# The gate and up products of a gated layer with the 64-row remainder of both weights side by side, and x^T by transposing DMAs

## The chip, the core and the metric

The kernel runs on one core of a Trainium2 chip. A core has engines with instruction streams of their own: TensorE (PE in the profile; its weight loads are PEld), VectorE (DVE), ScalarE (ACT), GpSimd (POOL) and SyncE (SP, which here only issues DMAs). They share the on-chip memory SBUF, with 128 partitions; TensorE writes its results to PSUM, 128 partitions by eight banks, each of which holds 512 f32 per partition. The metric is the device time of one execution in microseconds.

## The reference

The kernel computes an attention block with a cached K and V, multiplied by a gated layer, and all gradients. Cut to what matters here:

```python
x = A_x                                  # 1 x 2048 x 576
xn = _layernorm(x, axis=-1)
s = _A_ref(xn, k_cache, v_cache, wq, wo) # attention, 32 heads
def _B_ref(x, w_gate, w_up, w_down):     # 576 x 4608, 576 x 4608, 4608 x 576
    g = einsum("bsd,df->bsf", x, w_gate)
    u = einsum("bsd,df->bsf", x, w_up)
    h = sigmoid(g) * u
    return einsum("bsf,fd->bsd", h, w_down)
out = x + s * silu(_B_ref(xn, w_gate, w_up, w_down))
# returned: out and the gradients of x, k_cache, v_cache, wq, wo, w_gate, w_up, w_down
```

The change is in the first stage: the layer norm, xn transposed, g and u, and three results for later stages: a = sigmoid(g), h = a u, and b = h (1 - a), which the gradient needs.

## The kernel before

x has S = 2048 rows, 16 row tiles of 128 (`NT`); its D = 576 columns are four blocks of 128 and a remainder of 64 (`DT` = 5, `DL` = 4, `KL` = 64); the F = 4608 columns of Wg and Wu are nine chunks of 512 (`FCH`, `NFC`).

The first stage (lines 177 to 263 below):

- SP loads the first two tiles of x into `x_all`, the first chunk of `wg_sb` and `wu_sb` block by block of 128 rows, the other 14 tiles of x in one DMA (L197), then the further columns of both weights. `wg_sb` and `wu_sb` have five blocks each; of the fifth only 64 rows are data, and POOL zeroes the other 64 (`zpad`, L160), there and in `xnT`, so that every matmul uses all 128 rows.
- `ln_tile` (L206) normalizes a tile: statistics on DVE (L211, L213), the root on ACT (L215), its reciprocal and the bias on DVE, the normalization on ACT (L220), and then `transpose_to` (L53): five transposes on PE (L59), copied from PSUM to `xnT` by DVE (L42) and ACT (L40).
- The chunks run in three groups of three (`GRP`), within a group over the 16 tiles. For a tile and chunk there are five matmuls of 512 columns for g (L249) and five for u (L252); then two sigmoids of g on ACT (L253, L255) and two products on DVE (L256, L257). Each (tile, group) has three rows `a_row`, `b_row`, `h_row` that POOL stores by DMA to `a_d`, `b_d` and `h_d` (L259 to L263). PSUM holds three pairs of `g_ps` and `u_ps` (`a1ps`) and two banks for the transposes.
- POOL issues the store of xn and the load of `wd_sb`, the down projection's weights (L235, L236). `hT` of the first two tiles is read back from `h_d` by transposing DMAs in the last group (L261).

The order of instructions on each engine is the scheduler's here, not the program's: it may move an instruction ahead of others that it doesn't depend on. The load of `wd_sb`, for one, stands in the program at the last tile of the first group, and is issued 11 us into the execution.

The next stage (from L265) multiplies h by `wd_sb` (L306), with `hT` from transposing DMAs (`load_hT`, L279) into memory that the first stage's weights leave; `transpose_ds` (L266) later fills rows 64 to 127 of the last block of `xnT`. Much later a stage reads a, b and h again in blocks of columns (`load_abh`, L750) and computes another product with a 64-row remainder: `dh_main` (L782) and `dh_fifth` (L789), the latter with operands that alternate between rows 0 to 63 and 64 to 127.

Of the kernel before, what the change touches and what calls it, by code (L numbers as in the profile page):

```python
# [9 lines left out]
bf = mybir.dt.bfloat16  # L10
f32 = mybir.dt.float32
# [84 lines left out]
def kernel(  # L96
# [42 lines left out]
    a_d = dram.tile([S, F], bf, name="a_d")  # L139
    b_d = dram.tile([S, F], bf, name="b_d")  # L140
    h_d = dram.tile([S, F], bf, name="h_d")
# [9 lines left out]
    eps_t = pers.tile([P, 1], f32, name="eps_t")  # L151
    nc.vector.memset(eps_t[:], EPS)

    alt = Alt(nc)
    KPAD = dts[-1][1] < P
    d_last, kd_last = dts[-1]

    def zpad(t):
        if KPAD:
            nc.gpsimd.memset(t[kd_last:, DT - 1, :], 0.0)  # L160

    def kfull(i, kd):
        return P if KPAD else kd

    FCH = min(512, F)
    NFC = F // FCH
    GRP = ldiv(NFC, 3)
# [6 lines left out]
    zpad(xnT)  # L174
    dsT = pk.tile([P, DL, S], bf, name="dsT")
    wo_h = pk.tile([P, D], bf, name="wo_h")
    with tc.tile_pool(name="pa", bufs=1) as pa:
        wd_sb = pa.tile([P, FT, D], bf, name="wd_sb")
        with tc.tile_pool(name="a1w", bufs=1) as wp:
            a0x = tc.alloc_tile_pool(name="a0x", bufs=1, side="right")  # L180
            x_all = a0x.tile([P, NT, D], bf, name="x_all")
            XF = min(2, NT)
            nc.sync.dma_start(x_all[:, 0:XF, :], x2[0:XF * P, :].rearrange("(t p) d -> p t d", p=P))
            xn_st = x_all
            wg_sb = wp.tile([P, DT, F], bf, name="wg_sb")
            wu_sb = wp.tile([P, DT, F], bf, name="wu_sb")
            zpad(wg_sb)
            zpad(wu_sb)
            WSPL = GRP * FCH
            bounds = [0, FCH] + list(range(WSPL, F + 1, WSPL)) if WSPL > FCH else list(range(0, F + 1, WSPL))  # L190
            for bi in range(len(bounds) - 1):
                c0, c1 = bounds[bi], bounds[bi + 1]
                for i, (d0, kd) in enumerate(dts):
                    nc.sync.dma_start(wg_sb[:kd, i, c0:c1], B_w_gate[d0:d0 + kd, c0:c1])
                    nc.sync.dma_start(wu_sb[:kd, i, c0:c1], B_w_up[d0:d0 + kd, c0:c1])
                if bi == 0 and NT > XF:
                    nc.sync.dma_start(x_all[:, XF:, :], x2[XF * P:, :].rearrange("(t p) d -> p t d", p=P))  # L197
            FMAX = nc.vector.BN_STATS_FMAX
            nchunk = 1
            while D % nchunk != 0 or D // nchunk > FMAX:  # L200
                nchunk += 1
            with tc.tile_pool(name="a0", bufs=3) as sb0, tc.tile_pool(name="a0ps", bufs=2, space=PSUM) as ps0, \
                    tc.tile_pool(name="a1r", bufs=2) as rows, tc.tile_pool(name="a1t", bufs=3) as tmpp, \
                    tc.tile_pool(name="a1ps", bufs=3, space=PSUM) as ps:

                def ln_tile(st):  # L206
                    xt = x_all[:, st, :]
                    stats = sb0.tile([P, nchunk, nc.vector.BN_STATS_DIM], f32, name="stats")
                    xr = xt.rearrange("p (c f) -> p c f", c=nchunk)
                    for c in range(nchunk):  # L210
                        nc.vector.bn_stats(stats[:, c, :], xr[:, c, :])  # L211
                    mv = sb0.tile([P, nc.vector.BN_AGGR_DIM], f32, name="mv")
                    nc.vector.bn_aggr(mv[:], stats[:])  # L213
                    std = sb0.tile([P, 1], f32, name="std")
                    nc.scalar.activation(std[:], mv[:, 1:2], AF.Sqrt, bias=eps_t[:], scale=1.0)  # L215
                    nc.vector.reciprocal(rstd_all[:, st:st + 1], std[:])
                    xn_t = xn_st[:, st, :]
                    nbias = sb0.tile([P, 1], f32, name="nbias")
                    nc.vector.scalar_tensor_tensor(nbias[:], mv[:, 0:1], -1.0, rstd_all[:, st:st + 1], op0=ALU.mult, op1=ALU.mult)
                    nc.scalar.activation(xn_t, xt, AF.Identity, bias=nbias[:], scale=rstd_all[:, st:st + 1])  # L220
                    transpose_to(nc, ps0, xn_t, D, xnT, st * P, ident, alt)

                LA = 2
                for st in range(min(LA, NT)):
                    ln_tile(st)
                for grp in range(NFC // GRP):
                    if grp == 1:
                        a0x.release()
                        hp0 = tc.alloc_tile_pool(name="a2h0", bufs=1, side="right", reuse_waits="tile")
                        hT = {k: hp0.tile([P, FT, P], bf, name=f"hT{k}") for k in range(2)}  # L230
                    for st in range(NT):
                        if grp == 0 and st + LA < NT:
                            ln_tile(st + LA)
                        if grp == 0 and st == NT - 1:
                            nc.gpsimd.dma_start(xn_d[:, :].rearrange("(t p) d -> p t d", p=P), xn_st[:])  # L235
                            nc.gpsimd.dma_start(wd_sb[:], B_w_down.rearrange("(t p) d -> p t d", p=P))  # L236
                        srows = slice(st * P, (st + 1) * P)
                        a_row = rows.tile([P, GRP * FCH], bf, name="a_row")
                        b_row = rows.tile([P, GRP * FCH], bf, name="b_row")
                        h_row = rows.tile([P, GRP * FCH], bf, name="h_row")  # L240
                        for c in range(GRP):
                            fc = grp * GRP + c
                            fs = slice(fc * FCH, (fc + 1) * FCH)
                            cs = slice(c * FCH, (c + 1) * FCH)
                            g_ps = ps.tile([P, FCH], f32, name="g_ps")
                            u_ps = ps.tile([P, FCH], f32, name="u_ps")
                            for i, (d0, kd) in enumerate(dts):
                                kk = kfull(i, kd)
                                nc.tensor.matmul(g_ps[:], lhsT=xnT[:kk, i, srows], rhs=wg_sb[:kk, i, fs], start=(i == 0), stop=(i == DT - 1))  # L249
                            for i, (d0, kd) in enumerate(dts):  # L250
                                kk = kfull(i, kd)
                                nc.tensor.matmul(u_ps[:], lhsT=xnT[:kk, i, srows], rhs=wu_sb[:kk, i, fs], start=(i == 0), stop=(i == DT - 1))  # L252
                            nc.scalar.activation(a_row[:, cs], g_ps[:], AF.Sigmoid)  # L253
                            oma = tmpp.tile([P, FCH], bf, name="oma")
                            nc.scalar.activation(oma[:], g_ps[:], AF.Sigmoid, scale=-1.0)  # L255
                            nc.vector.tensor_tensor(h_row[:, cs], u_ps[:], a_row[:, cs], op=ALU.mult)  # L256
                            nc.vector.tensor_tensor(b_row[:, cs], h_row[:, cs], oma[:], op=ALU.mult)  # L257
# [766 lines left out]
```

## Time and profile before

| | |
|---|---|
| median of 3 runs | 5152.12 us (5147.52 to 5171.49) |
| the profiled execution | 5157.5 us as a run, 5155.7 us span |
| first matmul of g | 8.25 us |
| first matmul of the next stage (L306) | 349.16 us |
| TensorE busy, whole span | 4983.8 us, 97% |
| matmuls of g and u recorded (L249, L252) | 693 and 717 of 720 each |
| transposes of x on TensorE (L59) | 80 |

The profile is one execution. A row of a group of instructions gives the line, engine and operation, output and inputs with their shapes, the count, busy time and the mean length of one in ns, and then the idle time of the engine just before them and what ended it. A row of the order by time gives the start and length in us, and a count if equal instructions are merged. Matmuls are pipelined and overlap, so the pace is read from the distance of starts, not from the mean length. A DMA row gives the size and the median time from issue to landing.

### The profile page before, as it was taken

What the parts mean: (1) busy time and instruction counts of PE and PEld (TensorE: products, weight loads), DVE (VectorE), ACT (ScalarE), POOL (GpSimd) and SP (SyncE); (2) the same over time, 40 slices, a digit from 0 to 9 for tenths busy, and PEclk for the clock granted to TensorE, in tenths of its full rate; (3) what the DMA queues carried; (4) which work ended last, traced back from release to release, by engine and by line L of the source; (5) the groups of instructions that cost most, each with busy time, mean ns of one, the idle gap of its engine ahead of it and who ended that gap; (6) DMA issues with size and microseconds to landing.
All of it is one profiled execution on the core that took longest, in us unless ns stands there. A gap on an engine that the chain in (4) does not pass through costs nothing.

```text
span 5155.7 us, 124622 instructions
## 1 busy us (share of the span) xinstructions
PE 4983.8 (97%) x53232; PEld 3490.9 (68%) x54160; DVE 3231.5 (63%) x5070; ACT 2285.3 (44%) x2878; POOL 1388.1 (27%) x1981
## 2 busy tenths in 40 slices
PE   8999999999999999999999999999899999999999
PEld 3444777777777777777777777777655555554554
DVE  5545888888888888888888888888733222210101
ACT  6531665566556556655655665566501222100000
POOL 2222333233223323332332333233222222111000
PEclk9999999999999999999999999999999999999999
DMA  7478999999999999999999999999999776697775
GB/s 281 184 210 166 189 191 196 195 199 195 196 196 196 197 201 199 196 202 196 199 196 198 199 197 195 199 199 195 205 200 246 209 209 196 199 246 166 158 153 118
DMA packets 2710509, 1013.89 MB, mean 197 GB/s; under 512 B 2523360, under 2 KB 2643936, under 8 KB 2709952
## 3 DMA queue, kind: packets, MB, share of 16 engines
q1 hardware_dynamic: 2628256, 726.57, 81.9%
q0 software_dynamic: 81696, 279.29, 18.5%
q8 instruction: 423, 6.93, 0.5%
q14 instruction: 134, 1.10, 0.1%
HBM read 172.54 MB, written 201.00 MB: 72 GB/s over the span
## 4 chain that ended last, share of the span: by engine, by line
PE 84%; DVE 6%; DMA 5%; issue 4%; SPq 1%; ACT 0%; DVEq 0%; ACTq 0%; another core or an unknown queue 0%
PE acckv L544 17%; PE acc L525 14%; PE acc L965 8%; PE dp L495 6%; PE sp L465 5%; DVE sneg L467 5%; PE accp L424 5%; PE accw L848 5%; DMA dST<-dSq 3%; PE g_ps L249 3%; PE u_ps L252 3%; PE accd L833 3%; PE acc L306 3%; PE acc L903 2%; PE dh L782 2%
## 5 line engine op out<-in xcount | busy, mean ns | idle before, releaser
L476 ACT ACTIVATE Pq<-sneg,nm 128x2048 bf16<-128x2048 bf16 x512 | 1024.5, 2001 | 389.5 <-DVE sneg L467 386.4
L525 PE MATMUL acc<-Kn,dST 128*128 128x128 bf16 x8192 | 1066.6, 219 | 28.1 <-DMA dST<-dSq 26.1
L544 PE MATMUL acckv<-dOn,Pq 128*128 128x128 bf16 x8192 | 1032.1, 219 | 15.4 <-POOL negdelta L579 0.2
L525 PE MATMUL acc<-Vn,PT 128*128 128x128 bf16 x8192 | 1023.2, 219 | 10.9 <-DMA PT<-Pq 9.1
L498 DVE SCALAR_TENSOR_TENSOR dSq<-dp,delta,Pq 128x1024 bf16<-128x1024 f32 x608 | 773.9, 1281 | 351.6 <-PE dp L495 249.7
L544 PE MATMUL acckv<-Qn,dSq 128*128 128x128 bf16 x8192 | 897.7, 220 | 8.4 <-issue 0.2
L544 PEld LDWEIGHTS <-Pq 128*128 128x128 bf16 x8192 | 793.8, 98 | 117.6 <-issue 0.9
L525 PEld LDWEIGHTS <-dST 128*128 128x128 bf16 x8192 | 758.8, 98 | 162.9 <-DMA dST<-dSq 34.1
L525 PEld LDWEIGHTS <-PT 128*128 128x128 bf16 x8192 | 766.4, 98 | 151.2 <-DMA PT<-Pq 11.3
L544 PEld LDWEIGHTS <-dSq 128*128 128x128 bf16 x8192 | 719.7, 98 | 99.8 <-issue 0.3
L467 DVE TENSOR_SCALAR_CACHE_REDUCE sneg<-sp,nm 128x1024 bf16<-128x1024 f32 x512 | 656.5, 1282 | 83.8 <-PE sp L465 46.4
L467 DVE TENSOR_SCALAR_CACHE_REDUCE sneg<-sp 128x1024 bf16<-128x1024 f32 x512 | 625.1, 1221 | 60.4 <-PE sp L465 42.0
L501 ACT ACTIVATE t<-dp,negdelta 128x1024 bf16<-128x1024 f32 x416 | 463.6, 1114 | 425.7 <-PE acc L525 233.2
L465 PE MATMUL sp<-KT,QT 128*128 128x512 bf16 x1763 | 548.4, 380 | 33.0 <-DVE sneg L467 26.1
L495 PE MATMUL dp<-VT,dOT 128*128 128x512 bf16 x1728 | 540.4, 379 | 0.8 <-DVE dSq L498 0.8
L484 POOL TENSOR_TENSOR dOn<-dOn,rinv_all 128x256 bf16<-128x256 bf16 x256 | 155.9, 609 | 657.7 <-DVE rinv_all L480 540.6
L505 DVE TENSOR_TENSOR dSq<-t,Pq 128x1024 bf16<-128x1024 bf16 x416 | 319.5, 768 | 0.0
L848 PE MATMUL accw<-dd_blk,xn_all 128*128 128x512 bf16 x1134 | 250.6, 379 | 0.9
L978 DVE SCALAR_TENSOR_TENSOR junk<-dxn,xn_all 128x576 f32<-128x576 f32 x16 | 12.1, 758 | 368.2 <-ACT dxn L973 368.2
L965 PEld LDWEIGHTS <-cf 128*128 128x128 bf16 x2304 | 145.7, 98 | 142.7 <-DMA cf<-dg_d 4.5
L591 POOL DMA_DIRECT2D dq_d<-dq_n x128 | 98.7, 771 | 459.5 <-DVE dq_n L590 450.9
L848 PEld LDWEIGHTS <-xn_all 128*128 128x128 bf16 x1152 | 111.4, 98 | 133.8
(182 smaller groups left out, 6694.3 us busy)
## 6 DMA issues: line engine op xcount, KB each, us to landing
out_dram<-kv POOLq DMA_DIRECT2D x256, 128.0 KB, 5.2
h_d<-h_row POOLq DMA_DIRECT2D x48, 384.0 KB, 2.7
a_d<-a_row POOLq DMA_DIRECT2D x48, 384.0 KB, 2.6
b_d<-b_row POOLq DMA_DIRECT2D x48, 384.0 KB, 3.2
a_blk<-a_d SPq DMA_DIRECT2D x18, 1024.0 KB, 5.6
b_blk<-b_d SPq DMA_DIRECT2D x18, 1024.0 KB, 20.8
du_d<-dd_blk POOLq DMA_DIRECT2D x18, 1024.0 KB, 8.5
dg_d<-dd_blk POOLq DMA_DIRECT2D x18, 1024.0 KB, 11.5
```

Of the source, the lines that this page charges most:

```text
L424: nc.tensor.matmul(acc[:], lhsT=w[:, i, :], rhs=srcT[:, i, cs], start=(i == 0), stop=False)
L465: nc.tensor.matmul(sp[:, c * CH:(c + 1) * CH], lhsT=hs.QT[:, qs], rhs=hs.KT[:, hf * HW_ + c * CH: hf * HW_ + (c + 1) * CH], start=True, st ...
L467: nc.vector.tensor_scalar(sneg[:, hf * HW_:(hf + 1) * HW_], sp[:], -SCALE, None if hf == 0 else nm[:, hf - 1:hf], op0=ALU.mult, op1=ALU.mi ...
L476: nc.scalar.activation(Pq[:], sneg[:], AF.Exp, bias=nm[:, hf:hf + 1], scale=-1.0, accum_out=hs.rs_all[:, qt:qt + 1])
L495: nc.tensor.matmul(dp[:, c * CH:(c + 1) * CH], lhsT=hs.dOT[:, qs], rhs=hs.VT[:, hf * HW_ + c * CH: hf * HW_ + (c + 1) * CH], start=True, s ...
L498: nc.vector.scalar_tensor_tensor(dSq[:, hsl], dp[:], hs.delta[:, qt:qt + 1], Pq[:, hsl], op0=ALU.subtract, op1=ALU.mult)
L501: nc.scalar.activation(t[:], dp[:], AF.Identity, bias=hs.negdelta[:, qt:qt + 1], scale=1.0)
L505: nc.vector.tensor_tensor(dSq[:, hsl], t[:], Pq[:, hsl], op=ALU.mult)
L525: nc.tensor.matmul(bx.acc[:, j, :], lhsT=T[qt][:, kt, :], rhs=getattr(hs, rhs)[:, kt, :], start=(kt == 0), stop=(kt == NT - 1))
L544: nc.tensor.matmul(bx.acc[i][:, jj, :], lhsT=slabs[qt][:, k0:k0 + P], rhs=getattr(hs, rhs)[:, qt, :], start=(qt == 0 and jj == 0), stop=(q ...
L848: nc.tensor.matmul(acc[:], lhsT=xn_all[:, st, i * P:(i + 1) * P], rhs=dd_blk[:, st, :, :], start=(st == 0), stop=(st == NT - 1))
L965: nc.tensor.matmul(accs[sl][j][:, :nn], lhsT=ch[:, kk, sl * P:(sl + 1) * P], rhs=w_[:, n0:n0 + nn], start=(pi == 0 and kk == 0), stop=(las ...
```

## The change

The edits, all to the first stage but the last:

1. The remainders of Wg and Wu lie in one tile `wl_sb`: Wg's 64 rows in partitions 0 to 63, Wu's in 64 to 127. The normalized tile's last 64 columns are written twice (L202 after), so that the fifth block of `xnT` has them in both halves of its rows. `fifth` multiplies partitions 0 to 63 for g and 64 to 127 for u, one after the other, each with 64 rows; nothing is zeroed.
2. Chunks run in pairs, five groups (the last has one chunk, and takes two tiles at a time instead). A `Unit` is two (tile, chunk) results: g and u have two banks each. Two units A and B are worked together: `main(A)`, `fifth(A)`, `fifth(B)`, evict A, `main(B)`, evict B. Evictions, sigmoids and products, are 1024 columns wide.
3. Order on all five engines is the written one (`manual_schedule`).
4. Tiles 0 and 1 are transposed on PE and copied by ACT; tiles 2 to 15 by transposing DMAs that SP issues from `x_all` to `xnT`, in pairs (`ln_pair`), one pair of units ahead. SP's queue also carries the weights, two chunks after each of the first pairs of transposes, and after all of them `wd_sb`.
5. The layer norm's root is a power of -0.5 on POOL and its normalization is on DVE; ACT keeps one table.
6. a, b and h of a unit leave in one store to one tensor `abh_d`; the last group's in two.
7. Later stages read `abh_d` where they read `a_d`, `b_d`, `h_d`.

```diff
-    a_d = dram.tile([S, F], bf, name="a_d")
-    b_d = dram.tile([S, F], bf, name="b_d")
-    h_d = dram.tile([S, F], bf, name="h_d")
+    abh_d = dram.tile([3, S, F], bf, name="abh_d")
...
-    zpad(xnT)
...
+            x_all = a0x.tile([P, NT, DT * P], bf, name="x_all")
+            wg_sb = wp.tile([P, DL, F], bf, name="wg_sb")
+            wu_sb = wp.tile([P, DL, F], bf, name="wu_sb")
+            wl_sb = wp.tile([P, F], bf, name="wl_sb")
+            groups = [[c for c in (c0, c0 + 1) if c < NFC] for c0 in range(0, NFC, 2)]
+            with tc.tile_pool(name="a0", bufs=4) as sb0, tc.tile_pool(name="a1r", bufs=4) as rows, \
+                    tc.tile_pool(name="a1t", bufs=2) as tmpp, tc.tile_pool(name="a1ps", bufs=4, space=PSUM) as ps, \
+                    tc.manual_schedule(engines={mybir.EngineType.PE, mybir.EngineType.DVE, mybir.EngineType.Activation,
+                                                mybir.EngineType.SP, mybir.EngineType.Pool}):
...
+                def load_wgu(c0, c1):
+                    cs = slice(c0 * FCH, c1 * FCH)
+                    for k, (w, src) in enumerate(((wg_sb, B_w_gate), (wu_sb, B_w_up))):
+                        nc.sync.dma_start(w[:, :, cs], src[:DL * P, cs].rearrange("(t p) c -> p t c", p=P))
+                    for k, src in enumerate((B_w_gate, B_w_up)):
+                        nc.sync.dma_start(wl_sb[k * KL:(k + 1) * KL, cs], src[DL * P:, cs])
+
+                def ln_stat(st):
...
+                    nc.vector.tensor_scalar(vpe[:], mv[:, 1:2], EPS, None, op0=ALU.add)
+                    nc.gpsimd.tensor_tensor(rstd_all[:, st:st + 1], vpe[:], mhalf[:], op=ALU.pow)
...
+                def ln_norm(st):
+                    xt, mv = x_all[:, st, :], mvs.pop(st)
+                    nc.vector.tensor_scalar(xt[:, :D], xt[:, :D], mv[:, 0:1], rstd_all[:, st:st + 1], op0=ALU.subtract, op1=ALU.mult)
+                    nc.vector.tensor_copy(xt[:, D:], xt[:, DL * P:D])
...
+                def main(un, first, js=(0, 1)):
+                    for j in js:
+                        st, c = un.jobs[j]
+                        for acc, w in ((un.g, wg_sb), (un.u, wu_sb)):
+                            for i in range(DL):
+                                nc.tensor.matmul(acc[:, j, :], lhsT=xnT[:, i, st * P:(st + 1) * P], rhs=w[:, i, c * FCH:(c + 1) * FCH],
+                                                 start=(first and i == 0), stop=(not first and i == DL - 1))
+
+                def fifth(un, first, js=(0, 1)):
+                    for j in js:
+                        st, c = un.jobs[j]
+                        for k, acc in enumerate((un.g, un.u)):
+                            r = slice(k * KL, (k + 1) * KL)
+                            nc.tensor.matmul(acc[:, j, :], lhsT=xnT[r, DL, st * P:(st + 1) * P], rhs=wl_sb[r, c * FCH:(c + 1) * FCH],
+                                             start=first, stop=not first)
+
+                def out(un, parts=1):
+                    r_ = rows.tile([P, 3, 2, FCH], bf, name="abh")
+                    oma = tmpp.tile([P, 2, FCH], bf, name="oma")
+                    for k in range(parts):
+                        js = slice(k * 2 // parts, (k + 1) * 2 // parts)
+                        nc.scalar.activation(r_[:, 0, js, :], un.g[:, js, :], AF.Sigmoid)
+                        nc.scalar.activation(oma[:, js, :], un.g[:, js, :], AF.Sigmoid, scale=-1.0)
+                        nc.vector.tensor_tensor(r_[:, 2, js, :], un.u[:, js, :], r_[:, 0, js, :], op=ALU.mult)
+                        nc.vector.tensor_tensor(r_[:, 1, js, :], r_[:, 2, js, :], oma[:, js, :], op=ALU.mult)
+                    return r_
...
+                load_x(0, 1)
+                load_x(1, 2)
+                load_wgu(0, 1)
+                load_x(2, 4)
+                load_wgu(1, 2)
+                load_x(4, 8)
...
+                def ln_pair(st):
+                    for fn in (ln_stat, ln_norm):
+                        for k in range(2):
+                            fn(st + k)
+                    for k in range(2):
+                        cols = slice((st + k) * P, (st + k + 1) * P)
+                        nc.sync.dma_start_transpose(xnT[:, :, cols], x_all[:, st + k, :])
+                    if st == 2:
+                        load_x(8, NT)
+                    if st // 2 < len(groups):
+                        g = groups[st // 2]
+                        load_wgu(g[0], g[-1] + 1)
+
+                ln_pair(2)
+                for gi, grp in enumerate(groups):
...
+                    if gi == 1:
+                        nc.gpsimd.dma_start(xn_d[:, :].rearrange("(t p) d -> p t d", p=P), x_all[:, :, :D])
+                        nc.sync.dma_start(wd_sb[:], B_w_down.rearrange("(t p) d -> p t d", p=P))
...
+                    for n in range(0, len(units), 2):
+                        A, B = Unit(units[n]), Unit(units[n + 1])
+                        if gi == 0 and n == 0:
...
+                        else:
+                            main(A, True)
+                            fifth(A, False)
+                            fifth(B, True)
+                            ra = out(A)
+                            main(B, False)
+                        if gi == 0 and 2 <= n and n + 4 < NT:
+                            ln_pair(n + 4)
+                        rb = out(B, 2 if gi == len(groups) - 1 and n == len(units) - 2 else 1)
+                        if gi == 0 and n == 0:
+                            ln_pair(4)
+                        store(A, ra)
+                        store(B, rb)
+                        if gi == len(groups) - 1 and n == 2:
+                            for k in range(2):
+                                nc.sync.dma_start_transpose(hT[k][:], abh_d[2, k * P:(k + 1) * P, :])
```

139 lines of the change are left out of this document (52 added, 87 removed).

## The prediction

> **What bounds the kernel now.** I read the page first, then busy time by stage, then single lines and the written order of time in the first 350 us, the only stage the change rewrites.
>
> ```profile
> span 5155.7 us, 124622 instructions
> PE 4983.8 (97%) x53232; PEld 3490.9 (68%) x54160; DVE 3231.5 (63%) x5070; ACT 2285.3 (44%) x2878; POOL 1388.1 (27%) x1981
> PE 84%; DVE 6%; DMA 5%; issue 4%; SPq 1%; ACT 0%; DVEq 0%; ACTq 0%; another core or an unknown queue 0%
> ```
>
> TensorE (PE) carries 84% of the chain that ended last, so a PE slot saved in this stage should shorten the whole. The stages of the first 350 us (columns: length, PE busy and count, granted clock, DMA share, GB/s):
>
> ```profile
> 20.00:40.00 20.00, 14.10 (x51) 0.72 1.04 350
> 120.00:160.00 40.00, 39.84 (x187) 1.00 0.46 178
> ```
>
> From 120 us on PE never stops and DMA is half idle; until 40 us the DMA is full, PE waits, and its clock averages 0.72. So there are two regimes: matmul slots later, supply at the start. Ends and pace of the stage, by time (start, length, what):
>
> ```profile
> 8.25 1.89 PE L249 MATMUL g_ps<-wg_sb,xnT 128*128 128x512 bf16 x4
> ...
> 37.43 0.56 PE L59 MATMUL pt<-ident,x_all 128*128 128x128 bf16 x5
> 37.92 0.61 PE L252 MATMUL u_ps<-wu_sb,xnT 128*128 128x512 bf16 x2
> ...
> 336.21 1.24 PE L249 MATMUL g_ps<-wg_sb,xnT 128*128 128x512 bf16 x5
> 337.29 1.24 PE L252 MATMUL u_ps<-wu_sb,xnT 128*128 128x512 bf16 x5
> ...
> 349.16 1.11 PE L306 MATMUL acc<-wd_sb,hT 128*128 128x512 bf16 x7
> ```
>
> Five matmuls of 512 columns start 337.29 - 336.21 = 1.08 us apart in sum: 0.216 us a slot (the 1.24 holds the last one's modelled end). Five transposes occupy 0.49 us, 0.098 each. The stage runs from 8.25 to 349.16, 340.9 us. Its work is 16 tiles x 9 chunks x 10 matmuls = 1440 slots = 311.0 us, plus 70 transposes after the first ten, 6.9 us. The remaining 23.0 us are lost at the start.
>
> **The fifth product.** The 64-row remainder is now two matmuls on different halves of the rows. The trace has this form, 256 columns wide, in a later stage:
>
> ```profile
> 3906.20 1.91 PE L782 MATMUL dh<-wdT,doBT 128*128 128x256 bf16 x16
> 3907.95 0.44 PE L668 MATMUL pt<-ident,doB 128*128 128x128 bf16 x5
> ...
> 3943.25 3.67 PE L782 MATMUL dh<-wdT,doBT 128*128 128x256 bf16 x32
> 3946.85 1.05 PE L789 MATMUL dh<-wdT,doBT 64*128 64x256 bf16 x16
> 3947.83 3.34 PE L782 MATMUL dh<-wdT,doBT 128*128 128x256 bf16 x29
> ```
>
> Full ones: 16 in 1.75 us, 0.109 a slot. Then 32 should take 3.50; they take 3.60 up to the first half-row one. Sixteen half-row ones take 0.98; eight slots are 0.87. So two halves share one slot, and each change of form costs 0.10 us. Every half has its own weight load, here too, so that is in the price.
>
> A pair of units (four chunk results) was 40 slots. It becomes 32 full and 8 halves = 36 slots, and two changes, since the halves of A and B stand together: 7.78 + 0.20 = 7.98 us against 8.64. 36 pairs save 36 x 0.66 = **23.9 us**. Bounds: no sharing at 512 columns makes it 40 slots and 0.20, +7.2 us; free changes make it -31.1. I take the row, which is the same form at half the width.
>
> The rule that speaks against this: the Trainium skill, TensorEngine Tiling (Array Packing), Key Properties, says a change of tiling mode drains the TensorE. It gives no price. The trace agrees that there is one, 0.10 us; by an estimate of a drain as a matmul's full length less its slot (L782's 1.91 - 15 x 0.109 - 0.109 = 0.16 us), 72 changes would cost 11.5 instead of 7.2 us, and the gain would be 19.6.
>
> **Transposes off PE.** Tiles 2 to 15 no longer take PE slots: 70 x 0.098 = **6.9 us** saved. Nothing goes back on PE.
>
> **Evictions** are twice as wide and come in the order A, B. Rows of the same width:
>
> ```profile
> L501 ACT ACTIVATE t<-dp,negdelta 128x1024 bf16<-128x1024 f32 x416 | 463.6, 1114 | 425.7 <-PE acc L525 233.2
> L498 DVE SCALAR_TENSOR_TENSOR dSq<-dp,delta,Pq 128x1024 bf16<-128x1024 f32 x608 | 773.9, 1281 | 351.6 <-PE dp L495 249.7
> L505 DVE TENSOR_TENSOR dSq<-t,Pq 128x1024 bf16<-128x1024 bf16 x416 | 319.5, 768 | 0.0
> L988 DVE TENSOR_SCALAR t<-t,m,rstd_all 128x576 f32<-128x576 f32 x16 | 9.3, 578 | 0.6
> L211 DVE BATCH_NORM_STATS2 stats<-x_all 128x6 f32<-128x288 bf16 x32 | 12.9, 439 | 9.4 <-DMA x_all<-in_A_x_dram 9.4
> L213 DVE BATCH_NORM_AGGREGATE mv<-stats 128x2 f32<-128x12 f32 x16 | 3.1, 201 | 0.1
> L736 DVE COPY doB<-doB 128x64 bf16<-128x64 bf16 x16 | 2.9, 182 | 0.6
> ```
>
> Per unit of 3.99 us on PE: ACT 2 x 1.11 = 2.2, DVE 1.28 + 0.77 = 2.05. A's banks are free some 2.5 us after its fifth product, while B's 16 full matmuls run 3.46 us: hidden. In the first group DVE also normalizes two tiles per pair: four L211 (1.76), two aggregates and two small additions (0.7), two at L988's 0.58, two copies of 64 columns (0.36), in sum 4.0; with 4.1 of evictions that is 8.1 against PE's 7.98. Cover is nil there, and tile 4 is late: pair 0 ends at 8.25 + 0.2 + 1.7 (cold clock, below) + 7.98 = 18.1; B's eviction 3.2, statistics 2.5 and the first normalization 0.8 follow, so its transposing DMA is issued at 24.6 and, with some 4 us of landing, is there at 29, where 26.1 is wanted. Stall **3 us**.
>
> The power on POOL that replaces Sqrt has no row; between 0 and 1 us behind the second tile's statistics, taken as nothing. At the last unit the eviction in halves frees the banks of L306 before PE arrives; without that cover, 2.4 us.
>
> At nothing: the zeroing on POOL, and ACT's table loads (ACT is 44% busy); wd_sb, moved from POOL to SP behind all of x^T, wanted 200 us later (without that cover its 28.8 us, below); 80 stores for 144 on POOL; one tensor for a, b, h, read later in the same rows.
>
> **Supply in the first group** decides the rest. SP's queue now holds, in order: x tiles and chunks 0 and 1, transposes 2 and 3, x 8 to 15, then two chunks ahead of each further pair of transposes. A transpose waits there for DVE, and behind it wait weights that PE wants only in the next groups, then the next tiles. Rates (12 to 14 us: loads alone; 40 to 44: loads and stores), transposes back to back, and three landings:
>
> ```profile
> 12.00:14.00 2.00, 1.00 1.09 358
> 40.00:44.00 4.00, 1.00 1.05 416
> ...
> 613.40 28.09 SPq L513 DMA_TRANSPOSE PT<-Pq  x8
> ...
> PT<-Pq SPq DMA_TRANSPOSE x512, 5.7
> x_all<-in_A_x_dram SPq DMA_DIRECT2D x1, 288.0 KB, 2.9
> wd_sb<-in_B_w_down_dram POOLq DMA_DIRECT2D x1, 5184.0 KB, 28.8
> ```
>
> Eight transposes of 16 blocks in 28.1 us are 0.22 us a block; a tile of x has five, 1.1 us. Ahead of tile 6's landing lie x (2304 KB), six chunks of 1152 KB, together 9.4 MB, six tiles' transposes (6.6 us), and the stores of four units (768 KB each, 3.1 MB). At 387 GB/s, the middle, 12.5 MB take 32.4 us; with 2.5 us until data flows (the first x lands 2.9 after its issue at 0.7) and some 2 for the landing, 43.5. Pair 3 wanted it at 29 + 8 = 37: **6.5 us**. Up to tile 8: 2.4 MB of weights, 1.6 of stores, 2.2 us of transposes, 12.4 us against a pair's 8.0: **4.4**. Up to tile 10, half the weights: 9.3, **1.3**. After that 6.3, nothing. Gaps 3 + 6.5 + 4.4 + 1.3 = 15.2 us.
>
> PE slows after a stop:
>
> ```profile
> 51.63 2.29 PE L249 MATMUL g_ps<-wg_sb,xnT 128*128 128x512 bf16 x5 [3.06 <-ACT oma L255]
> 53.71 1.87 PE L252 MATMUL u_ps<-wu_sb,xnT 128*128 128x512 bf16 x5
> ...
> 55.42 1.24 PE L249 MATMUL g_ps<-wg_sb,xnT 128*128 128x512 bf16 x5
> ```
>
> Ten matmuls in 3.79 us instead of 2.16: 1.6 a stop. Three stops 4.8, the cold beginning 1.7, a start 0.2 later (the second tile's statistics stand ahead of the first tile's normalization). New loss 15.2 + 4.8 + 1.7 + 0.2 = 21.9 against 23.0: **-1.1**. Bounds: every transpose in time, only tile 4's stall and one slowdown, 6.5 (-16.5); each tile 2.5 us of queue time (rival 2), 38 (+15).
>
> **Sum.** -23.9 - 6.9 - 1.1 = -31.9 us. On the profiled execution's span 5155.7 (5157.5 as a run) that is 5123.8; the runs' median is 5152.1, 5.4 below that execution's run, so 5120.
>
> **Rivals.** (1) Supply in time: the queue is less full than I sum, loss 6.5, total -47.3, 5105. For: the load of wd_sb no longer competes early. Against: 9.4 MB is ahead of tile 6 anyway.
>
> (2) SP's queue gets less than its part beside the stores:
>
> ```profile
> 20.57 0.33 SPq L195 DMA_DIRECT2D wu_sb<-in_B_w_up_dram  x1
> 23.11 0.33 SPq L194 DMA_DIRECT2D wg_sb<-in_B_w_gate_dram  x1
> ```
>
> Each issue waits for an older load of 256 KB to land: 262 KB per 2.54 us is 103 GB/s while POOL's wd_sb ran, 0.29 of the 350 that all queues moved in that stage. If transposes fare so in the half of a pair that stores fill, and take 1.1 us in the other, a tile costs (3.8 + 1.1) / 2 = 2.5 us: 8.4 more up to tile 6, 2.8 each to tiles 8 and 10, 0.9 each to 12 and 14. Loss 38, total -16, 5136. The Trainium skill, DMA: Bandwidth & Descriptors, Queues, rings and completion order, has the rule: engines go round the queues packet by packet. The trace agrees as far as the 103 GB/s goes.
>
> (3) It doesn't do what it says: halves do not share a slot at 512 columns. +7.2 - 6.9 - 1.1 = -0.8, 5151. Against: L789.
>
> (4) Slower: the transposes do not overlap one another, and two of them per pair stand alone in SP's queue. The sign turns when the loss passes 23.0 + 30.8 = 53.8, at 1.1 + 31.9 / 14 = 3.4 us a tile. With the whole landing of a 16-block one, PT's 5.7 us, as each tile's time the loss grows by 14 x 4.6 = 64: +32, 5184. Against: the eight above follow at 3.5 us for three times the blocks.
>
> **Chances.** Forecast (gain 26 to 40) 0.50; (1) 0.20; (2) 0.17; (3) 0.05; (4) 0.08. A measurement tells 0.5%, 25.8 us, from no change. Faster: the first two less a little at the forecast's weak edge, 0.68; same: (2), (3) and that edge, 0.24; slower 0.08. The range reaches to (1) and as far below it as the lowest run lies below the median, 5105 - 5 = 5100, and to (2) and the profiled execution's distance above, 5136 + 6 = 5142.
>
> **What would show it.** Right: half-row matmuls in eights taking 0.97 us (4.5 slots) of PE; first L364 near 317; no PE idle after 110 us; transposes of tiles 6 and 8 landing near 43 and 56 with PE waiting on them, the weights of chunks 2 to 7 ahead. Wrong: eight halves taking 1.8 us; PE waiting on DVE or ACT past the first group; stops at every pair of the first group; a different length of any stage after the first.

## The result and the profile after

| | before | after |
|---|---|---|
| median of six runs each, side by side | 5166.6 us | 5132.1 us (5127.5 to 5142.1) |
| ratio | | 0.9945, 95% interval 0.9924 to 0.9966 |
| span of the profiled execution | 5155.7 us | 5125.3 us |
| first matmul of g | 8.25 | 7.27 |
| first matmul of the second stage (L306, now L364) | 349.16 | 320.55 |
| last matmul of the second stage, about | 494.2 | 478.6 |

The change makes the kernel faster by 0.55%, 28 us by the ratio (the medians lie 34.5 us apart), near the forecast of 32. The kernel before came out at 5166.6 us here, 14.5 above the 5152.1 from which the forecast was counted down to 5120; so it is the difference that was met, and 5132.1 lies 12 us above that number. The table's last rows say that this agreement is not made of the forecast's terms alone: the first stage ends 28.6 us earlier, but by the end of the second only 15.6 us are left. The profiled span fell by 30.4 us, so 14.8 us come from behind the second stage, where nothing was forecast. (Two runs below are left out of their kernels' medians, one of 8718 us with the single chunk in the middle and one of 5200 us, at a granted clock of 0.945, with late weights besides; the latter is the profiled one, so it is left out where places are compared too.)

The head of the page after the change, and its chain of waits by engine:

```profile
span 5125.3 us, 123935 instructions
PE 4952.3 (97%) x53164; PEld 3467.6 (68%) x54090; DVE 3212.2 (63%) x4928; ACT 2232.6 (44%) x2676; POOL 1368.6 (27%) x1929
...
PE 85%; DVE 6%; DMA 5%; issue 4%; SPq 0%; ACT 0%; POOL 0%; DVEq 0%; ACTq 0%
```

TensorE is busy 31.5 us less than before and still carries the chain. Now the pace of the stage, in the order of time (start, length, what):

```profile
206.38 0.39 PE L231 MATMUL g_ps<-wl_sb,xnT 64*128 64x512 bf16 x1
206.39 0.39 PE L231 MATMUL u_ps<-wl_sb,xnT 64*128 64x512 bf16 x1
...
207.35 1.04 PE L223 MATMUL g_ps<-wg_sb,xnT 128*128 128x512 bf16 x4
...
214.37 0.39 PE L231 MATMUL g_ps<-wl_sb,xnT 64*128 64x512 bf16 x1
```

A g half and a u half start 0.01 us apart, eight halves take 207.35 - 206.38 = 0.97 us, and a pair of units lasts 214.37 - 206.38 = 7.99 us. The forecast had 0.97 and 7.98. The stops of the stage, same view:

```profile
7.27 1.88 PE L223 MATMUL g_ps<-wg_sb,xnT 128*128 128x512 bf16 x4
...
31.79 1.89 PE L223 MATMUL g_ps<-wg_sb,xnT 128*128 128x512 bf16 x4 [5.96 <-DMA xnT<-x_all]
...
47.57 1.89 PE L223 MATMUL g_ps<-wg_sb,xnT 128*128 128x512 bf16 x4 [5.57 <-DMA xnT<-x_all]
...
58.89 1.04 PE L223 MATMUL g_ps<-wg_sb,xnT 128*128 128x512 bf16 x4 [0.47 <-DMA xnT<-x_all]
...
320.55 1.60 PE L364 MATMUL acc<-wd_sb,hT 128*128 128x512 bf16 x6 [5.78 <-ACT oma L240]
```

The bracket is PE's idle time and what ended it: x^T of tiles 4, 6 and 8 comes late, and PE stands once more, 5.78 us, at the door of the second stage. The second stage itself, before and after, by groups (busy time, mean ns, then idle time and its causes):

```profile
L306 PE MATMUL acc<-wd_sb,hT 128*128 128x512 bf16 x552 | 140.1, 380 | 0.0
```

```profile
L364 PE MATMUL acc<-wd_sb,hT 128*128 128x512 bf16 x552 | 144.1, 387 | 14.2 <-DMA hT<-abh_d 8.4 <-ACT oma L240 5.8
L364 PE MATMUL acc<-wd_sb,hT 128*128 128x64 bf16 x576 | 112.2, 195 | 1.6 <-issue 0.4
```

The same matmuls ran without a stop before. Now PE waits 8.4 us for hT inside the stage, and after the two stops its matmuls are longer, 387 ns for 380: the granted clock was 0.50 from 320 to 325 us and 0.66 from 345 to 355, against 1.00 from 360 to 370. The stage grew from 145.0 to 158.1 us. What happens ahead of its door, ScalarE by time and two DMA groups (KB each, median us from issue to landing) between 278 and 325 us:

```profile
310.93 1.02 ACT L239 ACTIVATE abh<-g_ps 128x1024 bf16<-128x1024 f32 x1 [3.03 <-DMA abh_d<-abh]
...
318.43 0.60 ACT L239 ACTIVATE abh<-g_ps 128x512 bf16<-128x512 f32 x1 [5.57 <-DMA abh_d<-abh]
```

```profile
abh_d<-abh POOLq DMA_DIRECT2D x15, 384.0 KB, 16.2
abh_d<-abh POOLq DMA_DIRECT2D x3, 768.0 KB, 3.7
```

The last sigmoids wait for a row buffer of `abh`, and that waits for a store. Stores of 768 KB land in 3.7 us; the half-size ones of the last group, which has a single chunk, need 16.2. While they are under way, two transposing loads of hT stand in SP's queue.

### The profile page after: what moved, and what is told of

Read it like the earlier page. It is cut to its first block, busy times and chain, and to the rows that moved or that the text cites. A ratio compares the mean times of both kernels' runs of the same rounds, so it can differ in the third digit from the quotient of the medians.

```text
span 5125.3 us, 123935 instructions
## 1 busy us (share of the span) xinstructions
PE 4952.3 (97%) x53164; PEld 3467.6 (68%) x54090; DVE 3212.2 (63%) x4928; ACT 2232.6 (44%) x2676; POOL 1368.6 (27%) x1929
## 3 DMA queue, kind: packets, MB, share of 16 engines
q14 instruction: 129, 1.06, 0.1%
## 4 chain that ended last, share of the span: by engine, by line
PE 85%; DVE 6%; DMA 5%; issue 4%; SPq 0%; ACT 0%; POOL 0%; DVEq 0%; ACTq 0%
PE acckv L602 17%; PE acc L583 15%; PE acc L1023 8%; PE dp L553 7%; PE sp L523 5%; DVE sneg L525 5%; PE accp L482 5%; PE accw L906 5%; PE accd L891 3%; PE acc L961 2%; PE acc L783 2%; PE acc L364 2%; PE dh L840 2%; PE g_ps L223 2%; PE acct L489 2%
## 5 line engine op out<-in xcount | busy, mean ns | idle before, releaser
L223 PEld LDWEIGHTS <-xnT 128*128 128x128 bf16 x1152 | 111.1, 99 | 161.0 <-issue 24.9
```

## The experiments

Three questions are open: whether two halves really share a slot, why tiles 4 and 6 are late, and what happens around the door of the second stage. Every ratio is against runs of the kernel before beside it, which had medians of 5166.6 to 5167.5 us. The changed kernel's own two medians, 5132.1 and 5123.7, lie 8 us apart, so a difference of that size between two kernels tells nothing. Behind the second stage, where these variants do not differ, single profiles spread by 27 us (shown at the end), so places are read from the two stages, and times from medians.

### The changed kernel once more

> The changed kernel as it is, beside the kernel before on one chip, to set the scale for the others. The first stage should again begin near 7.3 us and end (first L364) near 320.5, with PE stopped for some 6.1 us before tile 4's matmuls, 5.7 before tile 6's and 5.9 at the end of the stage. 30 to 35 us under the kernel before.

5123.7 us, ratio 0.9921 (0.9899 to 0.9944). The stops before tiles 4 and 6 are there again, 5.91 and 5.77 us. At the door PE waits 1.29 us in place of 5.78, with another 5.3 us for hT later; the second stage lasts 152.2 us. ScalarE waited for no store here. So the stops of the first group come back, and the wait at the door has a part of 1.3 us that needs no late store. The time, 41 us below by the ratio, is more than the 30 to 35 expected.

### Are the halves together? Written G first, then U

```diff
+def fifths(A, B):
+    for k in range(2):
+        r = slice(k * KL, (k + 1) * KL)
+        for un, first in ((A, False), (B, True)):
+            for j in range(2):
...
 main(A, True)
-fifth(A, False)
-fifth(B, True)
+fifths(A, B)
```

> The eight half-row matmuls of two units in another order: the four for g (partitions 0 to 63) one after the other, then the four for u (64 to 127). Theory (two halves share a slot only if neighbours in the order use different rows): 7 slots instead of 4, the eight take 1.62 us instead of 0.97, a pair of units 8.63 instead of 7.98 us; over 35 pairs 22.7 us more than the changed kernel. Rival (the gain comes from 64 rows being shorter work, in any order): no change, within 4 us.

5130.9 us, ratio 0.9921 (0.9890 to 0.9951): the 22.7 us do not appear. PE by time:

```profile
201.95 0.39 PE L240 MATMUL g_ps<-wl_sb,xnT 64*128 64x512 bf16 x1
201.96 0.39 PE L240 MATMUL u_ps<-wl_sb,xnT 64*128 64x512 bf16 x1
202.18 0.38 PE L240 MATMUL g_ps<-wl_sb,xnT 64*128 64x512 bf16 x1
202.19 0.38 PE L240 MATMUL u_ps<-wl_sb,xnT 64*128 64x512 bf16 x1
...
209.94 0.39 PE L240 MATMUL g_ps<-wl_sb,xnT 64*128 64x512 bf16 x1
```

In the program four g halves stand ahead of four u halves; in the trace they start in couples all the same, and the pair is 7.99 us as before. (The trace gives the starts alone; that the instructions reach TensorE in the written order follows from `manual_schedule`.) Alternation in the written order is not what makes them share, so this run did not take the sharing away, and the next one had to.

### Are the halves together? Kept apart by full matmuls

```diff
-main(A, True)
-fifth(A, False)
-fifth(B, True)
+for j, acc, w in ((0, A.g, wg_sb), (1, A.g, wg_sb), (0, A.u, wu_sb)):
+    half_main(A, j, acc, w, True)
+halves(A, 0, False)
+halves(B, 0, True)
+half_main(A, 1, A.u, wu_sb, True)
+halves(A, 1, False)
+halves(B, 1, True)
```

`halves(un, 0, ...)` holds the two half-row matmuls of a unit's g, `halves(un, 1, ...)` those of its u, and `half_main` four full ones.

> Same matmuls as the changed kernel, but four full-array matmuls of U stand between the four half-row matmuls of G and the four of U in every pair of units after the first, so that the two kinds can't be together however far TensorE brings them forward. Theory (a G half and a U half hold the array at the same time, and the pair is shorter by that): eight slots of 0.216 us in place of four and two more changes between tilings, 4 x 0.216 + 2 x 0.10 = 1.06 us a pair, so a pair of 9.05 us in place of 7.99 and stage 1 longer by 35 x 1.06 = 37 us: first matmul of stage 2 near 353 us, time near 5165, no better than before. Rival (the pair is shorter for another reason, say because a half-row matmul by itself takes half the time): a pair of 8.0 to 8.2 us, time as the changed kernel's, 5124 to 5132.

5160.5 us, ratio 0.9983 (0.9965 to 1.0000).

```profile
203.33 1.89 PE L244 MATMUL g_ps<-wg_sb,xnT 128*128 128x512 bf16 x8
205.06 1.03 PE L244 MATMUL u_ps<-wu_sb,xnT 128*128 128x512 bf16 x4
206.01 1.03 PE L238 MATMUL g_ps<-wl_sb,xnT 64*128 64x512 bf16 x4
206.98 1.04 PE L244 MATMUL u_ps<-wu_sb,xnT 128*128 128x512 bf16 x4
207.95 1.03 PE L238 MATMUL u_ps<-wl_sb,xnT 64*128 64x512 bf16 x4
...
212.38 1.89 PE L244 MATMUL g_ps<-wg_sb,xnT 128*128 128x512 bf16 x8
```

The same matmuls, now 9.05 us a pair, the number expected; the second stage begins at 349.6 us, where 353 was expected. Four halves alone take 206.98 - 206.01 = 0.97 us, as long as eight did together, change of form included. Nearly the whole gain is gone. That settles it: a half-row matmul by itself costs a full slot, and it is the sharing that pays.

### Weights out of the transposes' way

```diff
-if st // 2 < len(groups):
-    g = groups[st // 2]
-    load_wgu(g[0], g[-1] + 1)
+if st == 10:
+    load_wgu(groups[1][0], groups[1][-1] + 1)
+if st == 14:
+    for g in groups[2:]:
+        load_wgu(g[0], g[-1] + 1)
```

> The weights of groups 2 to 5 leave SP's queue ahead of the transposes: group 2's come after the transposes of tiles 10 and 11, the others after all. Theory A (the transposes of tiles 4 to 8 were late because the weights stand ahead of them in SP's queue): the stop before tile 4 falls from 6.1 to 1 to 3 us (DVE is then the last), the one before tile 6 from 5.7 to under 1, the slow clock behind them (2.1 and 2.7 us) goes with them; first L364 10 to 14 us earlier, near 308, time 10 to 14 us under the changed kernel. Rival B (the transposes are slow by themselves, or DVE is late): the stops stay within 2 us of what they were, and the time within 4 us of the changed kernel's. In both the stop at the end of the stage stays near 6 us.

5131.5 us, ratio 0.9939 (0.9917 to 0.9962). PE's stops here, then the transposes' landing from 12 to 36 us after the change and in this run:

```profile
27.66 1.61 PE L223 MATMUL g_ps<-wg_sb,xnT 128*128 128x512 bf16 x4 [2.48 <-DMA xnT<-x_all]
...
68.66 1.89 PE L223 MATMUL g_ps<-wg_sb,xnT 128*128 128x512 bf16 x4 [6.74 <-DMA xnT<-x_all]
```

```profile
xnT<-x_all SPq DMA_TRANSPOSE x5, 8.2
```

```profile
xnT<-x_all SPq DMA_TRANSPOSE x6, 5.2
```

The stop before tile 4 falls from 5.9 to 2.48 us, the one before tile 6 is gone; a new one stands before tile 12, behind the very weights that were moved there. The second stage starts at 311.4 us, 4.7 earlier than in the second measurement of the changed kernel, where 10 to 14 was expected. The transposes land sooner without the weights ahead of them, 5.2 us for 8.2. How much of the stop before tile 4 is the weights' is not settled by this one profile: a later run with none ahead, below, landed them in 5.7 us and still had a stop of 4.25. The time doesn't show the gain; the profile has 8.4 us of waits for hT, as the first one of the changed kernel.

### The single chunk third instead of last

```diff
 groups = [[c for c in (c0, c0 + 1) if c < NFC] for c0 in range(0, NFC, 2)]
+groups.insert(2, groups.pop())
```

> The group with a single chunk is the third instead of the last, so that the last group stores in 2 KB rows and the transposes of the first two hT come about 48 us before the stage ends. Theory C (at the end of the stage PE waits for the last eviction, which waits for a row buffer, whose store was held up by the transposes of hT): no wait of ACT for stores of abh over 1 us, PE passes into L364 without the stop of 5.9 us and without the slow clock behind it; 6 to 8 us under the changed kernel. Rival D (the wait is one for the banks alone, from the order of the last evictions): the stop stays above 3 us. The stops before tiles 4 and 6 stay within 1 us of 6.1 and 5.7.

5114.5 us, ratio 0.9912 (0.9885 to 0.9940). By groups, and the second stage as one stretch (length, then PE's busy time):

```profile
L365 PE MATMUL acc<-wd_sb,hT 128*128 128x512 bf16 x576 | 143.1, 380 | 1.3 <-ACT oma L241 1.3
L365 PE MATMUL acc<-wd_sb,hT 128*128 128x64 bf16 x576 | 111.0, 193 | 0.0
```

```profile
314.50:459.50 145.00, 144.96 (x1221) 76.64 (x1221) 68.45 (x107) 14.34 (x44) 36.11 (x44) 1.00 0.93 190
```

No wait for hT, none of ScalarE for a store, the clock back at 1.00, and the stage as long as before the change; 1.3 us at the door remain. Two more runs with the single chunk in the middle, below, say the same: the door's wait and the second stage's growth over 145.0 us are together 1.3 to 2.1 us in these three profiles, and 6.3 to 18.8 in the seven with the single chunk last and hT's loads on SP. So the last group's place is shown to cause most of what the door and the second stage gave back. The lowest of the seven, the run with G first, waited 4.6 us at the door and for no hT afterwards. The first group, untouched by this edit, stopped differently here: 4.99, 0.96, 4.56 and 0.59 us before tiles 4, 6, 8 and 10.

### Why the single chunk hurts: hT's loads later

```diff
-if gi == len(groups) - 1 and n == 2:
+if gi == len(groups) - 1 and n == len(units) - 2:
```

> The transposes of the first two hT are issued behind the last unit of the stage instead of behind its fourth; everything else is as in the changed kernel, the last group's stores of 1 KB rows too. Theory C (the stores of the last group are held up by the transposes of hT): stores of that group land in 3 to 5 us instead of a median of 16, ACT waits for no store over 1 us; PE then waits for hT itself instead, 8 to 15 us. Rival (rows of 1 KB make the stores slow by themselves): the stores still land in over 10 us and ACT still waits 5 us and more.

5144.6 us, one run. The edit did nothing where it aimed: the two loads started at 296.46 us, 23.4 ahead of the second stage, for 27.3 in the changed kernel, and the stores still took 14.3 us. SP has nothing else in its queue there, and the loads went out 3.0 us after the two stores that they read were issued (293.46 us), wherever the loads are written. So this run tells nothing for or against.

The same through ScalarE's queue, behind its last sigmoids:

```diff
-if gi == len(groups) - 1 and n == 2:
+if gi == len(groups) - 1 and n == len(units) - 2:
     for k in range(2):
-        nc.sync.dma_start_transpose(hT[k][:], abh_d[2, k * P:(k + 1) * P, :])
+        nc.scalar.dma_start_transpose(hT[k][:], abh_d[2, k * P:(k + 1) * P, :])
...
-nc.sync.dma_start_transpose(hT[k][:], abh_d[2, k * P:(k + 1) * P, :])
+(nc.scalar if k < 4 else nc.sync).dma_start_transpose(hT[k][:], abh_d[2, k * P:(k + 1) * P, :])
```

> As the changed kernel, but the first four transposing loads of hT are issued from ScalarE's queue behind its last activation of stage 1, so none of them can run beside the last stores of abh (written later on SP's queue, as tried before, they were issued just as early). Theory (the transposing loads hold up the 1 KB-row stores of the last group, and the wait for a row buffer at the end comes from that): the 384 KB stores land in 3 to 5 us in place of 14 to 17, ScalarE waits for no store, the first matmul of stage 2 is then late by the loads themselves, 10 to 20 us, all of it a wait for hT. Rival (the stores are slow by their own rows of 1 KB): landing stays at 11 to 17 us and ScalarE's wait of 2 to 6 us for a store stays.

```profile
abh_d<-abh POOLq DMA_DIRECT2D x16, 384.0 KB, 3.2
abh_d<-abh POOLq DMA_DIRECT2D x4, 768.0 KB, 3.7
```

```profile
L364 PE MATMUL acc<-wd_sb,hT 128*128 128x512 bf16 x550 | 141.0, 383 | 14.5 <-DMA hT<-abh_d 14.5
```

Without transposing loads beside them, the 384 KB stores land in 3.2 us instead of 16.2, and ScalarE waits for none. That decides it: it is the loads of hT that hold up the stores; the stores' short rows alone do not. It is no repair, since PE then waits the loads' 14.5 us (one run, 5144.5 us). With the single chunk in the middle the loads start 54 us before the door (260.7 and 314.5 us), where nothing is waiting for them yet.

### x^T on TensorE as before

```diff
-for k in range(2):
-    cols = slice((st + k) * P, (st + k + 1) * P)
-    nc.sync.dma_start_transpose(xnT[:, :, cols], x_all[:, st + k, :])
...
+if gi == 0 and n + 2 < NT:
+    transpose_x((n + 2, n + 3))
+    for k in range(3):
+        ps.tile([P, 2, 8, P], bf, name="pt", tag="b")
```

The three further tiles only take their turn, so that the units keep their places in PSUM.

> All tiles of x are transposed on PE and copied from PSUM by ACT; no transposing DMA in the first group. Price: 70 transposes, 6.9 us, and some 0.7 us per pair of waiting for the copy, 5 us. Gain if theory A holds: nothing on PE waits for SP's queue, so the stops before tiles 4 and 6 (6.1, 5.7) and the slow clock behind them (4.8) go, 16 us; 2 to 8 us under the changed kernel. If the transposing DMAs were not what stopped PE: 10 to 14 us over the changed kernel.

5135.6 us, ratio 0.9944 (0.9922 to 0.9967), so in time as the changed kernel. PE at the tiles' turns:

```profile
18.27 1.04 PE L223 MATMUL g_ps<-wg_sb,xnT 128*128 128x512 bf16 x4 [0.79 <-ACT xnT L210]
27.77 1.04 PE L223 MATMUL g_ps<-wg_sb,xnT 128*128 128x512 bf16 x4 [0.79 <-ACT xnT L210]
```

```profile
L365 PE MATMUL acc<-wd_sb,hT 128*128 128x512 bf16 x552 | 144.0, 387 | 5.2 <-ACT oma L240 3.0 <-DMA hT<-abh_d 2.2
```

No stop above 0.8 us. The second stage starts at 310.5 us; without the waits at the door, 3.0 here and 5.78 and 1.29 in the two profiles of the changed kernel, that is 307.5 against 314.8 and 314.8. So in this stage the transposing DMAs cost 7.3 us more in stops and slow clock than the PE time that they save; the two kernels with the single chunk in the middle (314.5 above, 309.3 below, 1.3 at both doors) give 5.2. The second stage was again long, 158.7 us, with the single chunk last: PE waits 2.2 us for hT there and 7.2 for DVE's `ds_t`.

### Repairs together

Late weights as above, with the single chunk in the middle:

> Both edits: the late weights and the single chunk in the third group. If theories A and C hold and don't touch each other, the gains add: 16 to 21 us under the changed kernel, about 47 to 55 us under the kernel before; first L364 near 300 to 303. If the stops were one supply limit that only moves (rival), less than 12 us.

5112.8 us, ratio 0.9899 (0.9870 to 0.9927), the lowest median, but 11 us below the changed kernel's second one where 16 to 21 were expected. No place is read from its profile, so what each edit adds in it stays open; the next kernel is another form of the same pair.

All weights from the second group on behind tile 15's transpose, and the single chunk in the middle:

```diff
+if st == 14:
+    for g in groups[1:]:
+        load_wgu(g[0], g[-1] + 1)
```

> Both repairs at once: all weights from the second group on are loaded only after tile 15's transpose is issued, and the single chunk's group runs third instead of last. The weights of the second group then go out near 65 us and are needed near 80, 2.4 MB at 330 GB/s being 7 us. Theory: the stop before tile 4 falls from 5.9 to about 2.5 us, the one before tile 6 from 5.8 to under 1 us, no new stop at 70 us, no wait for hT in the second stage: first matmul of stage 2 near 307, second stage 145 us, so its last hT matmul near 453 us against 468 to 479 in the changed kernel and 459.5 with the single chunk in the middle alone; time 5108 to 5115. Rival: the transposes are slow by themselves (a 16-bit transposing DMA of a tile takes long whether weights stand in the queue or not): stops of 4 to 5 us stay before tiles 4, 6 and 8, last hT matmul near 459, time 5117 to 5121.

5119.9 us, ratio 0.9912 (0.9887 to 0.9937).

```profile
29.33 1.45 PE L224 MATMUL g_ps<-wg_sb,xnT 128*128 128x512 bf16 x4 [4.25 <-DMA xnT<-x_all]
...
85.03 1.89 PE L224 MATMUL u_ps<-wu_sb,xnT 128*128 128x512 bf16 x4 [4.61 <-DMA wu_sb<-in_B_w_up_dram]
```

The stops before tiles 6 and 12 are gone; tile 4's is 4.25, not 2.5, and now the second group's weights are late. The second stage begins at 310.5 and ends at 456.4 us, 3 us ahead of the kernel with the single chunk in the middle alone. The time expected, 5108 to 5115, was missed; it lies in the rival's 5117 to 5121, though of the stops that the rival asked for only tile 4's is there.

x^T on TensorE, and the single chunk in the middle:

> The pairs of halves with the single chunk in the middle, and all of x transposed on TensorE as before the change, none by DMA. Theory (the transposing DMAs cost more in stops, 12 us, than the 70 x 0.098 = 6.9 us of TensorE time that they spare, and the slow second stage is the single chunk's place alone): no stop above 3 us in the first group, first matmul of stage 2 near 310, second stage 145 us, last hT matmul near 455; time 5110 to 5117, 2 to 8 us below the single chunk in the middle with transposing DMAs. Rival (in the run with transposes on TensorE the second stage was slow for another reason than the place of the single chunk): the second stage stays at 155 to 159 us and the time at 5125 to 5135.

5121.9 us, ratio 0.9909 (0.9887 to 0.9931). First matmul of the second stage at 309.3, its end at 454.3 us, the earliest of all, 24.3 us before the changed kernel's; the time expected, 5110 to 5117, was missed all the same. The second stage is back at 145.0 us, so its length in the run before was the single chunk's place, as the theory had it.

The four kernels with the single chunk in the middle have medians of 5113 to 5122 us and intervals that overlap, with one another and with the changed kernel's own second measurement. Which of them is best is not settled. That the single chunk belongs in the middle is seen in the second stage, not in the time.

## Why the prediction was right, and where not

**The fifth product: right, in mechanism and size.** 36 pairs at 7.99 us for 8.64 are 23.4 us, forecast 23.9. The run with the halves apart makes a pair 1.06 us longer with the same matmuls, 37 us over 35 pairs (its second stage starts 33 us later, waits at the door left out), so rival (3) is refuted directly, and a change of form is confirmed at 0.10 us: 9.05 - 7.99 = 4 x 0.216 + 2 x 0.10. The drain estimate of 0.16 us a change, which stood beside the rule of the Trainium skill, TensorEngine Tiling (Array Packing), Key Properties, would make it 1.18.

**The transposes: right on PE, dearer in supply.** They are gone from PE, 6.9 us, and rival (4) did not come. But the run with transposes on PE shows that this edit loses in its stage what it gains, and more.

**The start-up loss: near in sum, not in its parts.** The stage lasts 313.3 us and 36 pairs at 7.99 are 287.6, so 25.6 are lost. The stops before tiles 4, 6 and 8 are 6.0, 5.6 and 0.5, forecast 3, 6.5 and 4.4, with 1.3 at tile 10 that didn't come: 12.0 for 15.2. The slow beginning costs 2.4 (12 matmuls from 7.27 to 12.30 us, 2.6 at full pace; forecast 1.7); the forecast called it a cold clock, but the profile's granted clock is 1.00 from 8 to 12 us, so its cause stays open. The slow pace after stops took 2.1 and 2.7, 4.8 as forecast, with a granted clock of 0.50 from 32 to 36 us. The rest is the door, 5.8, and 0.6 not placed. The beginning came 1.0 us earlier, not 0.2 later. The step that failed for tile 4 was its landing. SP's queue after the change:

```profile
19.03 0.60 SPq L185 DMA_DIRECT2D wl_sb<-in_B_w_up_dram  x1
23.53 3.30 SPq L276 DMA_TRANSPOSE xnT<-x_all  x2
26.88 1.36 SPq L183 DMA_DIRECT2D wg_sb<-in_B_w_gate_dram  x1
...
34.24 8.77 SPq L276 DMA_TRANSPOSE xnT<-x_all  x2
```

The issue was worked out as 24.6 and was 23.5. The landing was taken as "some 4 us" and was 8.2; the second group's weights had been issued just ahead, up to 19.6 us, and without them it was 5.2 and 5.7. The stop was then 2.48 in one run, near the forecast's 3, and 4.25 in the other. The forecast counted these weights for tile 6 and not for tile 4. Rival (1) asked for a loss of 6.5 us, rival (2) for 38 with stops up to tile 14; neither came. That the sum of the stops is near is in part luck of the execution: three other profiles with the same first group stopped 17 to 19 us before tiles 4 to 8.

**The door: wrong.** "At the last unit the eviction in halves frees the banks of L306 before PE arrives" was priced at nothing. PE waits 1.3 us there in the quietest runs, for ScalarE's last sigmoid, and 5.8 in the profiled one. The 2.4 us given for the cover's loss did not foresee what takes the cover away: a late store that keeps a row buffer from ScalarE. Without any wait there the loss would be 19.8 us and the second stage would begin at 314.8; forecast were 21.7 (the 21.9 less its later start of 0.2) and 317, and with it they are 25.6 and 320.6.

**The second stage: wrong.** It was held to keep its length, and a different length of a later stage was one of the forecast's own signs of being wrong. It grew by 13.1 us (7.2 in the second measurement): 8.4 of waiting for hT and the slow clock behind it. The step that is missing is the order of the groups: the change puts a group of one chunk last, half as long, so hT's loads fall in its last 27 us, beside stores that they hold up. SP's queue before, then after:

```profile
256.13 18.49 SPq L261 DMA_TRANSPOSE hT<-h_d  x2
```

```profile
293.23 20.63 SPq L321 DMA_TRANSPOSE hT<-abh_d  x2
313.96 29.20 SPq L340 DMA_TRANSPOSE hT<-abh_d  x1
```

Before, the first two loads went out 93 us ahead of the door. The load that PE waits for inside the stage is the third, issued at 313.96 and landed 35.7 us later; with the single chunk in the middle no load took over 21.4. What in the crowd of stores and loads holds it up was not taken apart.

**The rest: not explained.** The profiled execution gained 14.8 us behind the second stage. PE's waits for transposing loads in between, before, after, and in the run with all weights late (us in total, times, longest):

```profile
PE acc L525 <- DMA dST<-dSq: 26.1, 24, 6.5
...
PE acc L525 <- DMA PT<-Pq: 9.1, 6, 3.6
```

```profile
PE acc L583 <- DMA dST<-dSq: 22.4, 16, 9.4
...
PE acc L583 <- DMA PT<-Pq: 4.8, 4, 2.1
```

```profile
PE acc L584 <- DMA dST<-dSq: 28.1, 14, 12.1
...
PE acc L784 <- DMA oT<-on_d: 14.7, 1, 14.7
```

They account for 8 of the 14.8 us, and they wander: in the changed kernel and its variants the stretch from the second stage's end to the stage of dh took between 3396 and 3423 us in eleven profiles, 3412 before. So in a single profile a gain of this size can be scatter. In the times it may not be all: the changed kernel lies 28 and 41 us lower by the ratios (34 and 44 by the medians), while the two stages end 15.6 and 25.9 earlier in the profiles beside them. Whether some 13 to 19 us come from something the change does later stays open. So the forecast's total was met partly by luck: an unforeseen loss of 13 us in the second stage met an unforeseen gain of 15 behind it.

## What to carry to other kernels

Two matmuls that each fill half of the array's rows cost one slot here when nothing of full height stood between them (eight in 0.97 us), and two when something did (four in 0.97 us); collect them, because each change of form cost 0.10 us as well. When work is taken off the bounding engine and given to a DMA queue, count what is already in that queue ahead of it, from the first tile on. When a loop's last round becomes shorter, look at what was timed by it: here the loads for the next stage moved from a quiet place to the stage's last 27 us, beside stores whose row buffers ScalarE waits for.

## What the runs showed of the hardware

- Four g halves written ahead of four u halves ran in couples, 0.01 us apart, at the same 7.99 us a pair: in these runs TensorE took half-row matmuls past at least the g halves in between that use the other rows. It did not take them past full matmuls (9.05 us).
- Transposing loads slowed plain stores far beyond their bytes. 384 KB stores took 16.2 us beside two of them and 3.2 without (11.1 to 14.4 in other runs with the loads beside them).
- The supply of the first group is not steady. With the same first group, the stop before tile 4 was 5.96, 5.91 and 4.99 us in three profiles and 11.4 to 14.0 in three others. PE at the longest of these, in the run with hT's loads written later, then a stretch of the run with G first (length, PE, PEld, DVE, ACT, POOL, clock, DMA share, GB/s):

```profile
38.47 1.89 PE L223 MATMUL g_ps<-wg_sb,xnT 128*128 128x512 bf16 x4 [13.98 <-DMA xnT<-x_all]
```

```profile
28.00:32.00 4.00, 0.00 (x0) 0.00 (x0) 2.96 (x7) 0.00 (x0) 1.75 (x3) 0.78 0.85 59
```

The DMA engines are busy 85% of those 4 us and move 59 GB/s, against 306 in the same stretch of the profiled changed kernel. What they were busy with was not found.
